# Three seams of a fused attention and two-MoE kernel: root chains moved, one product moved, the last eviction split

## The chip, the cores and the metric

The kernel runs on one core of one Trainium2 chip. The metric is device time in microseconds (us) of one execution, as a median over runs of the same program. TensorE is called PE here, VectorE DVE, ScalarE ACT, GpSimd POOL, and SyncE, which issues the DMAs, SP.

## The reference

```python
B, H, S, D = 4, 8, 576, 64            # q, k, v; 4 * 576 = 2304 tokens, 8 * 64 = 512 features
k_p, v_p = k and v averaged over groups of 8 positions
attn = softmax(q @ k_p.T / sqrt(D))
x = (attn @ v_p) as [2304, 512]
rms = sqrt(mean(x * x, axis=-1) + 1e-6)
xn = x / rms * rms_g
x = (silu(xn @ w_gate) * (xn @ w_val)) @ w_out        # first stage, 512 -> 1536 -> 512
out = ((x @ w_a) * (x @ w_b)) @ w_out2                # second stage, 512 -> 1536 -> 512
```

All inputs and the output are float32; the weights arrive as float64 words and are narrowed on the chip.

## The kernel before

The matrix products run in a rounded 32-bit format. An operand is split into a high part (a cast, on ACT) and a low part (a subtraction, on DVE or POOL), and a product is three matmuls: high by low, high by high, low by high. The matmuls of the large products have 512 columns.

**First stage.** The 2304 tokens are cut into five tiles of 512, 256, 512, 512 and 512 tokens, called tiles 1 to 5 here. A tile runs 12 blocks, one per 128 of the 1536 hidden features. A block is 12 matmuls for the gate `g` (L649), 12 for the value `v` (L649), and the output product `acc` of the block before (L662, 12 matmuls; in tile 2 L670, 8 matmuls). ACT turns `g` into `ht` by silu (L1233). DVE multiplies it by `v` (L1241), which frees the one PSUM bank of `v`. ACT casts it to `hh` (L1250), and DVE subtracts to `hl` (L1251). `ht` has one buffer from tile 3 on. Behind the last block stand two output products in a row, those of blocks 10 and 11 (blocks count from 0), and then the first `g` of the next tile, whose input `xf` is split into `xh` and `xl` (L635, L636) as soon as the last `v` has read the old ones.

**The attention beside it.** The attention of the next tile is worked in steps between these matmuls, in units of 256 tokens. Steps `A5` to `A8` are scores and softmax, `V3` to `V8` the products with the values. A unit ends in a root chain: PE sums the squares (`sq` by L445, or `ms` by L515 and L516), DVE finds the inverse root in three Newton steps (L478 to L493), and scales `xf` by it (L529). In tile 2 the root is found in a narrow form, made into a diagonal matrix `dg` (L464) and spread by PE (`rb`, L472) ahead of the scaling. There the order of the steps is a written list, `SECOND`; in tiles 3 and 4 a list of steps, `SIDE`, is dealt out evenly over 48 places, four for each block (L1206 to L1211). Until tile 5 a scheduler then places each instruction on its engine; in tile 5 and the second stage they stand as they are written.

**Second stage.** Seven products per group (`group`, L1030) go through banks X, Y and Z. The last product of a group, which adds into X, is put off into the next group (`flush`, L1064). `out_block` (L1110) multiplies the hidden features, read back from DRAM, by `w_out2`: for each of the first ten feature blocks three matmuls into each of six banks, then the last two blocks bank by bank, each bank evicted to `ev` and stored (L1136 to L1145). The very last `flush` stands in the first out_block, behind the second bank.

Of the kernel before, what the change touches and what calls it, by code (L numbers as in the profile page):

```python
# [17 lines left out]
P = 128  # L18
UNIT = 256
TILES1 = [512, 256, 512, 512, 512]  # L20
SLICE = 768
# [25 lines left out]
""".split()  # L47
SECOND = """
A4.0 =r0 -r1 r2 -r3 r4 -r5 V3.0 r7 =r6 =r8 -V3.1 =V3.2 N0 =V3.3 A4.1 -N1
=A4.2 A4.3 A4.4 =V3.4 V3.5 -A4.5 =V4.0 . =V4.1 =V3.6 -V4.2 =V4.3 V4.4 V4.5 V3.7 =V4.6  # L50
. =V4.7 . . .
""".split()


# [9 lines left out]
def attention_moe_moe2(  # L64
# [14 lines left out]
    nc = tc.nc  # L79
# [32 lines left out]
    for t0, n in starts(TILES1):  # L112
# [9 lines left out]
        out=mask, in_=mask, pattern=[[P, NV], [-SP, H]], compare_op=ALU.is_ge,  # L122
# [3 lines left out]
        out=mask, in_=mask, pattern=[[-P, NV], [SP, H]], compare_op=ALU.is_ge,  # L126
# [412 lines left out]
    def merge(*lists):  # L539
        keyed = []  # L540
        for order, steps in enumerate(lists):
            for i, st in enumerate(steps):
                keyed.append(((i + 0.5) / len(steps), order, i, st))
        return [st for _, _, _, st in sorted(keyed, key=lambda r: r[:3])]
# [134 lines left out]
    def dest(u):  # L679
        t = u * UNIT  # L680
        for idx, (t0, n) in enumerate(starts(TILES1)):
            if t0 <= t < t0 + n:
                def get():
                    if idx not in xf_t:
                        new_xf(idx)
                    return xf_t[idx][:, :, t - t0:t - t0 + UNIT]
                return get

    A = [score_steps(u) for u in range(NU)]
    V = [value_steps(u, dest(u)) for u in range(NU)]  # L690
    loads, prep = zip(*(prep_steps(b) for b in range(B)))
# [60 lines left out]
    for u in range(5):  # L752
# [3 lines left out]
    SIDE = [  # L756
        [],
[lambda t=t: token(t) for t in SECOND],
        A[5] + list(prep[2][9:]) + prep[3] + merge(A[6], V[5]) + V[6],
        A[7] + merge(A[8], V[7]) + V[8],  # L760
    ]

    def token(t):
        behind = t[0] if t[0] in "-=" else ""
        key, _, banks = t.lstrip("-=").partition("@")
        boot["alt"] = key[-1] == "!"
        key = key.rstrip("!")
        boot["banks"] = banks.split(",") if banks else []
        boot["on"] = key[0] in "kwtx" or key[:2] in ("A0", "A1", "V0", "V1")
        run(names[key], behind)  # L770
        boot["on"] = False
        boot["banks"] = []
        boot["alt"] = False
# [71 lines left out]
    NS2 = NT // SLICE  # L845
# [164 lines left out]
    def bank(name):  # L1010
        return two["ps"].tile([P, 512], F32, tag="bank", name=name, bufs=8)
# [52 lines left out]
    def flush():  # L1064
        if not pending:
            return
        f, s, X, c00 = pending.pop()
        product(X, f, A11, s, "t4", False, True)
        nc.vector.tensor_mul(c00, c00, X[:, :HALF])
        store(f, s, 0, c00)  # L1070
# [32 lines left out]
    def prepare():  # L1103
        if todo:
            s, f = todo.pop(0)
            if s == 0:
                out_weights(f)
            hidden_of(s, f)

    def out_block(s):  # L1110
        accs = []

        def add(f, i):
            if f == 0:
                accs.append(bank(f"o_{s}_{i}"))
            wh, wl = WO[f]
            hh, hl = HO[s, f]
            sub = slice(i * P, (i + 1) * P)
            for j, (x, y) in enumerate(((hh, wl), (hh, wh), (hl, wh))):
                nc.tensor.matmul(  # L1120
                    accs[i], x[:, sub], y, start=(f == 0 and j == 0), stop=(f == NF - 1 and j == 2),
                )

        NA = SLICE // P
        for f in range(NF - 2):
            for i in range(NA):
                add(f, i)
                if f == 0 and s == 0 and i == 1:
                    flush()
                    later.close()  # L1130
                    two["r"] = ctx.enter_context(
                        tc.tile_pool(name="o3", bufs=1, side="right", reuse_waits="tile")
                    )
            prepare()
        prepare()
        for i, acc in enumerate(accs):  # L1136
            for f in range(NF - 2, NF):
                add(f, i)
            ev = two["o"].tile([P, 512], F32, tag="ev2", name=f"ev_{s}_{i}", bufs=3)
            if i % 2 == 0:  # L1140
                nc.scalar.copy(ev, acc)
            else:
                nc.vector.tensor_copy(ev, acc)
            t0 = s * SLICE + i * P
            nc.sync.dma_start(out=out[t0:t0 + P, :], in_=ev)  # L1145
        prepare()

# [2 lines left out]
    def second_phase():  # L1150
# [37 lines left out]
        for s in range(NS2):  # L1188
            out_block(s)

    last_act = [None]
    for idx, (ph, t0, n) in enumerate(work):
# [70 lines left out]
        for c, acc in enumerate(accs):  # L1263
            if last_tile:
                if c == 0:
                    last_x = x_p.tile([P, KD, 512], F32, tag="xf", name="last_x")
                ev = last_x[:, c]
            else:
                ev = ev_p.tile([P, 512], F32, tag="ev", name="ev")
# [45 lines left out]
```

## Time and profile before

| | |
|---|---|
| median of 3 runs | 1023.58 us (1022.65 to 1023.66) |
| the profiled execution, its own time | 1024.57 us |
| its span, first to last instruction | 1022.80 us |
| PE busy | 980.8 us, 96% of the span |
| DVE, ACT, POOL busy | 612.5, 451.7 and 399.6 us |
| mean granted PE clock | 0.985 of full speed |
| chain that ended last | PE 81%, DVE 12%, DMA 3%, issue 2%, ACT 1% |

The chain that ended last is followed back from the last instruction, each step to what released it. It is on PE for most of the span, so what can be won lies where PE waits, where it runs at half its clock, and in what follows its last matmul. Such places are found in the table of PE's waits, in the stretches with their granted clock, and in the timeline. A matmul's printed end is modelled: while PE runs without a pause, 512-column matmuls start 0.23 us apart and are printed as 0.39 us long.

### The profile page before, as it was taken

The numbers are of one execution on the slowest core, as the hardware profiler recorded it, in microseconds if no ns is written. First come the engines' busy times: TensorE is split into PE (matmuls) and PEld (weight loads), VectorE is DVE, ScalarE is ACT, GpSimd is POOL, SyncE is SP. The second block draws the span as 40 slices with busy tenths as digits, with TensorE's granted clock in tenths as the row PEclk, the third lists the DMA queues.
The fourth block names the chain that finished last, engine by engine and source line by source line (L and its number), as shares of the span: only waits on it lengthen the run. The fifth ranks groups of instructions, "written<-read, shape, count | busy, mean of one in ns | idle before, by whom it ended". The sixth has DMA issues, their size and how long they took to land.

```text
span 1022.8 us, 13568 instructions
## 1 busy us (share of the span) xinstructions
PE 980.8 (96%) x4920; PEld 845.7 (83%) x4920; DVE 612.5 (60%) x966; ACT 451.7 (44%) x848; POOL 399.6 (39%) x324
## 2 busy tenths in 40 slices
PE   4988999999999989999999999999999999999998
PEld 3776676788888877888788899999999999888886
DVE  6898966775634764463628759766776665222221
ACT  3845662454535445444445445444444434321211
POOL 6476672533343433343348611533344333310000
PEclk9889999999999999999999999999999999999999
DMA  8556544320100001000111133443444345643431
GB/s 228 156 175 195 176 141 107 113 70 1 42 8 14 1 6 57 1 1 1 42 44 60 42 115 128 125 160 119 148 146 127 126 137 183 193 136 124 140 115 67
DMA packets 82802, 101.55 MB, mean 99 GB/s; under 512 B 24112, under 2 KB 63024, under 8 KB 82736
## 3 DMA queue, kind: packets, MB, share of 16 engines
q1 hardware_dynamic: 82736, 100.69, 31.7%
q8 instruction: 39, 0.64, 0.3%
q14 instruction: 27, 0.22, 0.1%
HBM read 73.93 MB, written 26.74 MB: 98 GB/s over the span
## 4 chain that ended last, share of the span: by engine, by line
PE 81%; DVE 12%; DMA 3%; issue 2%; ACT 1%; SPq 0%; DVEq 0%; ACTq 0%
PE o L1120 15%; PE X L1019 14%; PE v L649 10%; PE g L649 10%; PE acc L662 9%; PE Y L1019 7%; PE acc L670 4%; PE Z L1019 3%; PE xT L399 2%; PE g L799 2%; PE v L799 2%; PE sc L318 1%; DVE wf L596 1%; DVE wf L599 1%; DMA kv<-in_k_dram 1%
## 5 line engine op out<-in xcount | busy, mean ns | idle before, releaser
L621 POOL TENSOR_TENSOR wl<-wf,wh 128x512 fp32r<-128x512 f32 x144 | 193.6, 1351 | 242.6 <-ACT wh L620 230.3
L620 ACT CAST wh<-wf 128x512 fp32r<-128x512 f32 x156 | 94.9, 618 | 77.9 <-PE v L649 31.8
L1098 DVE TENSOR_TENSOR hl<-hf,hh 128x768 fp32r<-128x768 f32 x36 | 34.3, 958 | 95.5 <-ACT hh L1097 95.4
L1120 PE MATMUL o<-woh,hl 128*128 128x512 f32 x216 | 85.8, 397 | 0.0
L1120 PE MATMUL o<-woh,hh 128*128 128x512 f32 x216 | 85.0, 393 | 0.0
L1120 PE MATMUL o<-wol,hh 128*128 128x512 f32 x216 | 84.7, 392 | 0.0
L606 POOL TENSOR_TENSOR w<-w,st 128x512 int32<-128x512 int32 x24 | 31.9, 1328 | 115.8 <-DVE w L599 114.6
L649 PE MATMUL v<-xh,wl 128*128 128x512 f32 (+1 forms) x192 | 72.7, 379 | 1.8 <-DVE ht L1241 1.8
L649 PE MATMUL g<-xh,wl 128*128 128x512 f32 (+1 forms) x192 | 73.0, 380 | 0.0
L649 PE MATMUL g<-xh,wh 128*128 128x512 f32 (+1 forms) x192 | 70.2, 366 | 0.0
L649 PE MATMUL g<-xl,wh 128*128 128x512 f32 (+1 forms) x192 | 70.2, 366 | 0.0
L649 PE MATMUL v<-xl,wh 128*128 128x512 f32 (+1 forms) x192 | 69.9, 364 | 0.0
L649 PE MATMUL v<-xh,wh 128*128 128x512 f32 (+1 forms) x192 | 69.7, 363 | 0.0
L1097 ACT CAST hh<-hf 128x768 fp32r<-128x768 f32 x36 | 29.8, 834 | 89.8 <-PE o L1120 83.0
L670 PE MATMUL acc<-ht,wf 128*128 128x256 f32 (+1 forms) x208 | 67.5, 466 | 1.2 <-DVE ht L813 0.7
L606 POOL TENSOR_TENSOR wf<-wf,st 128x512 int32<-128x512 int32 x36 | 52.9, 1476 | 39.0 <-DVE wf L599 17.3
L1241 DVE TENSOR_TENSOR ht<-ht,v 128x512 f32<-128x512 f32 (+1 forms) x48 | 29.6, 617 | 64.1 <-PE v L649 60.0
L662 PE MATMUL acc<-hh,wl 128*128 128x512 f32 x144 | 57.5, 399 | 3.8 <-ACT hh L1250 3.8
L1233 ACT ACTIVATE ht<-g 128x512 f32<-128x512 f32 (+1 forms) x48 | 26.1, 544 | 77.8 <-PE g L649 71.7
L662 PE MATMUL acc<-hl,wh 128*128 128x512 f32 x144 | 57.0, 396 | 0.1
L1027 ACT COPY p<-X 128x384 f32<-128x384 f32 x36 | 17.2, 478 | 90.2 <-PE X L1019 90.2
L662 PE MATMUL acc<-hh,wh 128*128 128x512 f32 x144 | 56.8, 394 | 0.0
(208 smaller groups left out, 2713.2 us busy)
## 6 DMA issues: line engine op xcount, KB each, us to landing
hf<-h SPq DMA_DIRECT2D x36, 384.0 KB
st<-in_moe_w_out_dram SPq DMA_DIRECT2D x24, 512.0 KB
h<-u SPq DMA_DIRECT2D x36, 192.0 KB
h<-p SPq DMA_DIRECT2D x36, 192.0 KB
st<-in_moe_w_gate_dram SPq DMA_DIRECT2D x12, 512.0 KB
st<-in_moe_w_val_dram SPq DMA_DIRECT2D x12, 512.0 KB
st<-in_moe_w_a_dram SPq DMA_DIRECT2D x12, 512.0 KB
st<-in_moe_w_b_dram SPq DMA_DIRECT2D x12, 512.0 KB
```

What stands on the lines that cost most here:

```text
L606: nc.gpsimd.tensor_tensor(out=bits, in0=bits, in1=low, op=ALU.add)
L620: nc.scalar.copy(wh, wf[ph, f, i])
L621: (nc.vector if boot["alt"] else nc.gpsimd).tensor_sub(wl, wf[ph, f, i], wh.bitcast(F32))
L649: nc.tensor.matmul(bank[:, :n], w[:, c, :], x[:, c, cols], start=(i == 0), stop=(i == 3 * KD - 1),)
L662: nc.tensor.matmul(accs[c][:, cols], w[:, c, :], x[:, :n], start=(f == 0 and i == 0 and cols.start == 0), stop=(f == NF - 1 and i == 2),)
L670: nc.tensor.matmul(accs[c][:, cols], wf[0, f, 2][:, c, :], ht[:, :cols.stop - cols.start], start=(f == 0 and cols.start == 0), stop=(f == ...
L799: nc.tensor.matmul(bank[:, :n], w[:, c, :], x[:, c, cols], start=(c == 0 and i == 0), stop=(c == KD - 1 and i == len(terms) - 1),)
L1019: nc.tensor.matmul(dst[:, :HALF], w[:, c0 + c, :], x[:, c, :], start=(start and i == 0), stop=(stop and i == 5), skip_group_check=True,)
L1097: nc.scalar.copy(hh, hf)
L1098: nc.vector.tensor_sub(hl, hf, hh.bitcast(F32))
L1120: nc.tensor.matmul(accs[i], x[:, sub], y, start=(f == 0 and j == 0), stop=(f == NF - 1 and j == 2),)
L1241: nc.vector.tensor_mul(ht[:, :m], ht[:, :m], vb[:, :m])
```

## The change

It has three parts. In tile 2 the last two units' steps trade places in the written list: the sum of unit 4 (`V4.6`) now stands ahead of the scaling of unit 3 (`V3.7`), and the scaling of unit 4 (`V4.7`) one place later. In tiles 3 and 4 six empty steps are put behind the list, so that 48 and 36 steps become 54 and 42 over the same 48 places. In the first out_block the last `flush` stands behind the third bank instead of the second. The last eviction of all is done in halves of 256 columns, the first by ACT, which also issues its store, the second by DVE with SP's store. In the changed program DVE's half waits for ACT's.

```diff
 SECOND = """
 A4.0 =r0 -r1 r2 -r3 r4 -r5 V3.0 r7 =r6 =r8 -V3.1 =V3.2 N0 =V3.3 A4.1 -N1
-=A4.2 A4.3 A4.4 =V3.4 V3.5 -A4.5 =V4.0 . =V4.1 =V3.6 -V4.2 =V4.3 V4.4 V4.5 V3.7 =V4.6
-. =V4.7 . . .
+=A4.2 A4.3 A4.4 =V3.4 V3.5 -A4.5 =V4.0 . =V4.1 =V3.6 -V4.2 =V4.3 V4.4 V4.5 =V4.6 V3.7
+. . =V4.7 . .
 """.split()
...
-        A[5] + list(prep[2][9:]) + prep[3] + merge(A[6], V[5]) + V[6],
-        A[7] + merge(A[8], V[7]) + V[8],
+        A[5] + list(prep[2][9:]) + prep[3] + merge(A[6], V[5]) + V[6] + [lambda: None] * 6,
+        A[7] + merge(A[8], V[7]) + V[8] + [lambda: None] * 6,
...
-                if f == 0 and s == 0 and i == 1:
+                if f == 0 and s == 0 and i == 2:
                     flush()
...
+            t0 = s * SLICE + i * P
+            if s == NS2 - 1 and i == NA - 1:
+                nc.scalar.copy(ev[:, :256], acc[:, :256])
+                nc.scalar.dma_start(out=out[t0:t0 + P, :256], in_=ev[:, :256])
+                nc.vector.tensor_copy(ev[:, 256:], acc[:, 256:])
+                nc.sync.dma_start(out=out[t0:t0 + P, 256:], in_=ev[:, 256:])
+                continue
```

On PE in tile 2, blocks 10 and 11, before (`rb` spreads the root of a unit, `sq` sums the squares of unit 4; `acc` is the output product):

```order
L670 MATMUL acc_1555<-ht,wf_0_8_1085 128x256
L472 MATMUL rb_2183<-dg_2065,ones 128x256
L649 MATMUL g<-xh,wl_2133 128x256
...
L445 MATMUL sq_2203<-ones,ss_2098 128x2 x2
L649 MATMUL v<-xh,wl_2175 128x256
...
L670 MATMUL acc_1555<-ht,wf_0_9_1190 128x256
L472 MATMUL rb_2243<-dg_2221,ones 128x256
L649 MATMUL g<-xh,wl_2200 128x256
```

The same place now:

```order
L670 MATMUL acc_1555<-ht,wf_0_8_1085 128x256
L445 MATMUL sq_2183<-ones,ss_2098 128x2 x2
L649 MATMUL g<-xh,wl_2133 128x256
...
L472 MATMUL rb_2221<-dg_2065,ones 128x256
L649 MATMUL v<-xh,wl_2175 128x256
...
L670 MATMUL acc_1555<-ht,wf_0_9_1190 128x256
L649 MATMUL g<-xh,wl_2218 128x256
...
L472 MATMUL rb_2265<-dg_2201,ones 128x256
L649 MATMUL v<-xh,wl_2240 128x256
```

The sum `sq` moved ahead by the 12 gate matmuls of block 10, and the last `rb` moved behind the 12 gate matmuls of block 11.

On DVE at the end of tile 3, before (`sl` is the low part of the squares that PE sums into `ms`, `nr` the root, `xf` the next tile's input):

```order
L508 CAST sh_3273<-ss_3149 128x256
L1241 TENSOR_TENSOR ht<-ht,v 128x512
L509 TENSOR_TENSOR sl_3274<-ss_3149,sh_3273 128x256
L1251 TENSOR_TENSOR hl<-ht,hh 128x512
L478 TENSOR_SCALAR ss_3149<-ms_3294 128x256
...
L529 TENSOR_TENSOR xf_2750<-xf_2750,nr_3297 128x4x256
L1241 TENSOR_TENSOR ht<-ht,v 128x512
L636 TENSOR_TENSOR xl<-xf_2750,xh 128x512 x2
L1251 TENSOR_TENSOR hl<-ht,hh 128x512
```

The same place now:

```order
L508 CAST sh_3202<-ss_3078 128x256
L509 TENSOR_TENSOR sl_3203<-ss_3078,sh_3202 128x256
L1247 TENSOR_TENSOR ht<-ht,v 128x512
L478 TENSOR_SCALAR ss_3078<-ms_3220 128x256
...
L529 TENSOR_TENSOR xf_2707<-xf_2707,nr_3223 128x4x256
L1247 TENSOR_TENSOR ht<-ht,v 128x512
L1257 TENSOR_TENSOR hl<-ht,hh 128x512
L1247 TENSOR_TENSOR ht<-ht,v 128x512
L636 TENSOR_TENSOR xl<-xf_2707,xh 128x512 x2
L1257 TENSOR_TENSOR hl<-ht,hh 128x512
```

One pair of `ht` and `hl` more stands between the scaling and the split of `xf`: the chain moved ahead by a block. On PE its sum `ms` stood behind `v` of block 10 and the output product after it; now it stands right behind `v` of block 9, which is 48 matmuls of 512 columns earlier. In tile 4 `ms` stood in the middle of `v` of block 10; now it stands ahead of `g` of block 9, 54 matmuls earlier, and three pairs of `ht` and `hl` follow the scaling. Early in tile 4, ACT now has the exponent of unit 7's softmax, with a table load on either side, ahead of the silu of block 1; it stood behind it.

## Rows read from the trace of the kernel before

**Rows 1.** Waits of PE by what ended them: total us, times, longest us

```profile
PE rb L472 <- DVE dg L464: 4.9, 3, 2.0
...
PE acc L662 <- ACT hh L1250: 3.8, 2, 3.3
...
PE eT L367 <- DVE e L342: 1.7, 2, 1.0
PE X L1019 <- DVE p L1058: 1.4, 1, 1.4
```

**Rows 2.** Windows: us, busy (instructions) by engine, PEclk, DMA share, GB/s

```profile
254.10:257.40 3.30, 3.30 (x15) 3.12 (x15) 1.22 (x1) 0.00 (x0) 0.00 (x0) 0.50 0.00 0
380.40:383.70 3.30, 3.30 (x10) 2.48 (x9) 2.25 (x4) 1.61 (x3) 1.60 (x1) 0.50 0.14 55
```

**Rows 3.** PE timeline, end of tile 2: start us, us, engine, line, instruction

```profile
246.34 0.59 PE L472 MATMUL rb<-dg,ones 128*128 128x256 f32 x2
...
248.19 0.50 PE L445 MATMUL sq<-ones,ss 128*128 128x2 f32 x4
...
253.96 1.07 PE L472 MATMUL rb<-dg,ones 128*128 128x256 f32 x2 [2.00 <-DVE dg L464]
...
257.40 0.34 PE L649 MATMUL v<-xh,wl 128*128 128x256 f32 x1
```

**Rows 4.** Timeline of DVE, the last root chain of tile 2

```profile
248.73 0.16 DVE L478 TENSOR_SCALAR ba<-sq 128x4 f32<-128x4 f32 x1 [0.54 <-PE sq L445]
...
253.33 0.48 DVE L464 TENSOR_SCALAR dg<-ident,br 128x128 f32<-128x128 f32 x2
```

**Rows 5.** Timeline of PE at the seam of tiles 3 and 4

```profile
365.46 0.39 PE L662 MATMUL acc<-hh,wl 128*128 128x512 f32 x1
...
368.19 0.28 PE L515 MATMUL ms<-sl,ones 128*128 128x256 f32 x1
...
376.36 0.39 PE L662 MATMUL acc<-hl,wh 128*128 128x512 f32 x1
380.01 0.47 PE L662 MATMUL acc<-hh,wl 128*128 128x512 f32 x1 [3.26 <-ACT hh L1250]
...
384.43 0.39 PE L649 MATMUL g<-xh,wl 128*128 128x512 f32 x1
```

**Rows 6.** Timeline of DVE, the last root chain of tile 3

```profile
368.63 0.42 DVE L478 TENSOR_SCALAR ss<-ms 128x256 f32<-128x256 f32 x1 [0.24 <-PE ms L516]
...
372.55 1.55 DVE L492 TENSOR_TENSOR y<-y,ss 128x256 f32<-128x256 f32 x1
...
376.95 1.22 DVE L529 TENSOR_TENSOR xf<-xf,nr 128x1024 f32<-128x1024 f32 x1
```

**Rows 7.** Timeline of POOL, the low part of one split weight

```profile
372.53 1.29 POOL L621 TENSOR_TENSOR wl<-wf,wh 128x512 fp32r<-128x512 f32 x1 [2.01 <-ACT wh L620]
```

**Rows 8.** Timeline of PE at the seam of tiles 4 and 5

```profile
496.95 0.47 PE L662 MATMUL acc<-hh,wl 128*128 128x512 f32 x1 [0.51 <-ACT hh L1250]
...
500.16 0.39 PE L649 MATMUL g<-xh,wl 128*128 128x512 f32 x1
```

**Rows 9.** Timeline of PE where the out-projection begins

```profile
865.14 0.40 PE L1120 MATMUL o<-wol,hh 128*128 128x512 f32 x1
...
865.84 0.40 PE L1120 MATMUL o<-wol,hh 128*128 128x512 f32 x1
```

**Rows 10.** Timeline of all engines at the end

```profile
1018.74 0.69 DVE L1143 COPY ev<-o 128x512 f32<-128x512 f32 x1 [2.10 <-PE o L1120]
1019.46 0.33 SPq L1145 DMA_DIRECT2D out_dram<-ev  x1
```

**Rows 11.** Groups by form, half-wide evictions, busy us, mean ns

```profile
L1273 DVE COPY ev<-acc 128x256 f32<-128x256 f32 x2 | 0.8, 418 | 1.9 <-PE g L649 1.9
...
L1271 ACT COPY ev<-acc 128x256 f32<-128x256 f32 x2 | 0.7, 366 | 1.8 <-DMA x<-ev 1.8
```

**Rows 12.** DMA in 40 slices of 1018 to 1023 us: GB/s

```profile
GB/s 410 181 0 0 0 82 295 442 344 426 360 148 0 0 0 0 0 0 197 410 360 426 360 312 33 0 0 0 0 0 0 0 0 0 0 0 0 0 0 0
```

More of the change, by code (lines that the diff above doesn't have):

```diff
@@ L1143, in out_block @@
                 nc.vector.tensor_copy(ev, acc)
-            t0 = s * SLICE + i * P
             nc.sync.dma_start(out=out[t0:t0 + P, :], in_=ev)
```

## The prediction

> **What bounds the kernel now.** I read the chain that ended last first: PE carries 81% of it, and PE is busy for 96% of the span, so a change gains only where PE waits, runs slowly, or has finished. Then the table of PE's waits, for the four that touch the edited places [rows 1]: the last spreading `rb` of tile 2 waits 2.0 us for the diagonal matrix `dg`, an output product at the end of tile 3 waits 3.3 us for `hh`, a transpose early in tile 4 waits 1.0 us for the softmax, and the last `flush` waits 1.4 us for DVE to read bank X. Third, the windows with the granted clock [rows 2]: right behind the waits of tiles 2 and 3 PE was granted 0.50, which is 1.2 of 2.4 GHz. So these two waits cost their idle time and a slow stretch besides. Last, the timelines of PE and DVE around each place.
>
> A printed idle counts from a modelled end. Matmuls that follow without a pause start 0.23 us apart, since three take 0.70 us [rows 9], but are printed as 0.39 us long [rows 5]; so I add 0.16 us to an idle.
>
> **Tile 2.** The last `rb` waits 2.00 + 0.16 = 2.16 us. From its start at 253.96 to the first value matmul at 257.40 it and 12 gate matmuls take 3.44 us; the same work before it, 246.34 to 248.19, took 1.85 us [rows 3]. The slow clock thus cost 1.59 us, and the place 3.75 us. Nothing is added or removed by the trade: `sq`, both `rb` and both scalings remain. The sum `sq` moves from 248.19 to 246.34, 1.85 us earlier. Its DVE chain, L478 at 248.73 to the end of `dg` at 253.81, is 5.08 us [rows 4]; with the scaling of unit 3 now in its middle (1.22 us, the length of L529 [rows 6]) it would end at 248.73 - 1.85 + 5.08 + 1.22 = 253.2. The last `rb` moves behind the gate of block 11. Without the wait that gate starts at 253.96 - 2.16 = 251.8 and takes about 1.6 us, so `rb` is due at 253.4. The wait goes, with 0.2 us to spare; were the chain 1.3 us longer by one POOL split, 1.1 us of the 3.75 would return. Next in line are the splits `xh` and `xl`, which lie beside two output products and were waited for by nobody. I take 3.75, range 2.65 to 3.75.
>
> **The end of tile 3.** PE waits 3.26 + 0.16 = 3.42 us at 380.01. The 12 matmuls from there to 384.43 take 4.42 us, an ordinary output product 2.73 us (365.46 to 368.19), so the slow clock and restart cost 1.69 us [rows 5]. Together 5.11 us. The cause stands in DVE's queue: the root chain holds DVE from 368.63 to 378.17, 9.54 us [rows 6], and block 11's `ht` is queued behind it, though its `v` had long been done. In the new order the sum stands 48 matmuls earlier, 48 x 0.227 = 10.9 us. Even with one more pair of `ht` and `hl` in it (0.7 us each, as a 512-wide DVE pass [rows 10]) the chain ends near 378.2 - 10.9 + 1.4 = 368.7, ahead of the end of the last `v`, which lies one output product ahead of 376.6, at 373.9. What is late next is the ordinary sequence `ht`, `hh`, `hl`, three passes of 0.7 us, beside block 10's output product of 2.73 us: hidden. I take the whole 5.11.
>
> **The end of tile 4.** The wait is 0.51 + 0.16 = 0.67 us for `hh`; from 496.95 to 500.16 the product takes 3.21 instead of 2.73 us, as `hl` is late too [rows 8]. That is 1.15 us. The chain moves by 54 matmuls, 12.2 us, and the whole is gained.
>
> **Inside tiles 3 and 4.** The same attention steps, with the same instructions, now fill about seven eighths of the places. The transpose's wait early in tile 4 was 1.0 + 0.16 = 1.16 us. The exponent now runs ahead of the silu, so the softmax is ready sooner; but that silu and the weight casts behind it come later, and the low part that POOL makes for the gate of block 2 (1.29 us [rows 7]) may be what PE waits for instead. Bounds: 1.16 us gained to 0.13 lost (1.29 in place of 1.16). I take 0.4 gained, nearer the loss because both ends of that trade stand on the path.
>
> In tile 3 the sum `ms` now follows right behind a `v`. Its input leaves PE 2.72 us earlier, and two ACT and three DVE operations lie between, about 0.4 us each with their hand-overs, about 2.3 us. One DVE operation that meets a POOL split would make PE wait: at 372.55 L492 took 1.55 us where its neighbours took 0.42, and POOL's split ran from 372.53 to 373.82 [rows 6, 7]. Between 0 and 1.29 us; I take 0.45 lost. By the Trainium skill's page "SBUF — State Buffer", section "Who interferes with whom", a DVE operation with two SBUF inputs and a GpSimd operation that reads SBUF take turns for a whole instruction; the row agrees. By that rule a block has three splits to meet wherever the chain stands, so moving it cannot shorten it and 0.45 stays; without it this loss would be nil.
>
> For smaller waits of this kind at the other moved steps I take 0.3 lost, between 0 and 1.3 (one more split on the path).
>
> **The last flush.** The wait ends when DVE has read X, which does not depend on the third projection bank. Three matmuls, 0.70 us [rows 9], move into a wait of 1.4 + 0.16 = 1.56 us. The operands of the third bank are those of the first two, so it waits for nothing new. Gain 0.70; 0.86 us of wait remains.
>
> **The last eviction.** Before: DVE's copy from 1018.74, 0.69 us, then the store's issue at 1019.46 [rows 10]; the bytes move in slices 18 to 24 of the 40, 1020.25 to 1021.1 [rows 12]. Now ACT's half takes 0.37 us and DVE's 0.42 us [rows 11], one after the other since DVE's half waits for ACT's, with a hand-over of about 0.05: the second store is issued 0.37 + 0.05 + 0.42 - 0.69 = 0.15 us later. But only half of the bytes, about 0.4 of 0.85 us, still have to move then. Net gain 0.25. The trace shows no DMA issued by ACT; bounds are 0.4 gained (no hand-over, no wait between the halves) and 1.6 lost (ACT's store takes longer by as much as a whole one of SP's, from issue to last byte, 1019.46 to 1021.1). I take 0.25, as a store of the same kind is the nearest row.
>
> By the Trainium skill's page "PSUM — Partial Sum Buffer", section "PSUM bank collisions raise a hardware error", two engines must not be in one PSUM bank at a time, two readers included. No row here shows two readers in one bank. By that rule the halves cannot overlap, and the gain is the 0.25 above; if they could, it would be 0.28 + 0.4, some 0.7.
>
> **The sum.** 3.75 + 5.11 + 1.15 + 0.4 + 0.70 + 0.25 = 11.36 gained, 0.45 + 0.3 = 0.75 lost: 10.6 us net. PE is the bound to the end, so what is won early is kept. Against the profiled execution's own 1024.57 that gives 1013.9. The profile ran 1.0 us above the median of the runs, 1023.58, and against that median it is **1012.9 us**.
>
> **Rivals.**
> *The middle pays.* Fuller places make PE wait inside tiles 3 and 4 at three to five new spots of about 1 us, one of them long enough for another slow stretch of 1.6 us: 4 us lost in all, 1016.9. For it: DVE and POOL hold each other up, and steps of one chain now stand closer. Against it: the transpose's 1.0 us is the only wait of PE above 0.2 us that its table has inside tiles 3 and 4 [rows 1], with the same steps nearly as close.
> *The slow stretches stay.* If the clock falls at those places for another reason than the idle time, only the idle is won: 1012.9 + 1.59 + 1.69 = 1016.2. Against it: both stretches begin within 0.5 us of the end of a wait of more than 2 us.
> *The chain goes ahead of the gate* (slower). The moved chains stand ahead of the next block's `ht` in DVE's queue, and `v` has one bank. If a chain outlasts the time to the next `v` (13.6 us in tile 3, 10.9 us in tile 4, counted in matmuls of 0.227 us from `ms`), PE stops for `v` and falls to half its clock: 2.2 to 3.4 us and 1.6 us at each of the four root chains, 15 to 20 us in all, less the 10.6: 1028 to 1033, about 1030. It turns the whole to a loss only when all four overrun. The chain of tile 3 took 9.5 us with three meetings with POOL, so each would need two to four more.
> *It does not do what it says.* The scheduler could leave the steps where they were: 1023. The order shows them moved, so only an equal wait elsewhere could bring this.
>
> **Chances.** Forecast 0.72, the middle pays 0.16, slow stretches stay 0.05, slower 0.03, no effect 0.04. The forecast's own range is 1010.8 to 1015: with every uncertain term at its good end it is 0.75 + 0.75 + 0.15 = 1.65 lower, 1011.3, less half of the runs' spread of 1.0, 1010.8; with the bad ends of tile 2 (1.1) and of the inside (0.5 + 0.85) nearly 1015 is reached, less than all of 2.45 being likely at once. With the middle-pays case the range is 1010.8 to 1016.9. A measurement of this kernel can tell 0.2%, about 2 us, from no change. Faster takes the first three cases, 0.93; same 0.04; slower 0.03.
>
> **What would show it.** Right: no wait of PE above 1 us at the last `rb` of tile 2 and at the two seams, no stretch near half the granted clock behind the first 100 us, the wait at the last `flush` near 0.8 us, and the last store's bytes ending about 0.3 us nearer to PE's last matmul. Wrong: a PE wait for `ms`, `wl` or `v` of over 2 us inside tiles 3 and 4, or a slow stretch there; or a first ACT store that takes microseconds longer than SP's.

## The result, and the profile after

The changed kernel takes 1012.6 us as a median (1011.5 to 1014.5), against 1023.6 us for the kernel before on the same chip: a ratio of 0.9892, with a 95% interval of 0.9875 to 0.9908, or 11.0 us. On a second chip the ratio was 0.9890 (0.9872 to 0.9908). The forecast was 1012.9 us within 1010.8 to 1016.9.

The profiled execution took 1014.52 us, with a span of 1012.75 us, 10.05 us less than the span of before. These are the rows of its page that answer to the table of before: instructions and busy time of PE, and the granted clock in 40 equal slices.

```profile
span 1012.8 us, 13575 instructions
...
PE 976.4 (96%) x4920; PEld 842.3 (83%) x4920; DVE 610.0 (60%) x966; ACT 452.0 (45%) x849; POOL 402.9 (40%) x324
...
PEclk8799999999999999999999999999999999999999
```

Behind the first two slices no slice is below 9. The table of PE's waits (total us, times, longest us) answers to [rows 1]:

```profile
PE rb L472 <- DVE dg L464: 3.0, 2, 2.0
...
PE X L1019 <- DVE p L1058: 0.7, 1, 0.7
...
PE eT L367 <- DVE el L380: 0.3, 1, 0.3
```

The wait for `hh` is gone from the table. One of the three waits for `dg` is gone; the two that are left lie in the first tile. The long wait for `e` early in tile 4 is gone, a new one of 0.3 us for `el` has come, and the `flush` waits half as long. The windows at the three seams, in the columns of [rows 2], show the full clock:

```profile
253.70:257.00 3.30, 3.30 (x24) 3.11 (x23) 2.07 (x3) 1.97 (x5) 1.29 (x1) 1.00 0.01 2
371.50:374.80 3.30, 3.30 (x16) 2.75 (x15) 3.06 (x6) 3.30 (x7) 0.05 (x1) 1.00 0.01 2
485.00:488.30 3.30, 3.30 (x17) 2.72 (x16) 3.14 (x6) 2.57 (x5) 0.00 (x0) 1.00 0.00 0
```

PE at the end of tile 2 answers to [rows 3]:

```profile
245.36 1.89 PE L670 MATMUL acc<-ht,wf 128*128 128x256 f32 x8
247.09 0.50 PE L445 MATMUL sq<-ones,ss 128*128 128x2 f32 x4
...
253.98 0.59 PE L472 MATMUL rb<-dg,ones 128*128 128x256 f32 x2
...
259.10 0.58 PE L649 MATMUL g<-xh,wl 128*128 128x512 f32 x1
```

The last `rb` waits for nothing. From this `acc` (244.61 before, 245.36 now) to the first gate of tile 3 (262.14, 259.10) it is 13.74 us instead of 17.53. DVE has `dg` ready 2.0 us ahead of the `rb`, in the chain that answers to [rows 4]:

```profile
247.63 0.16 DVE L478 TENSOR_SCALAR ba<-sq 128x4 f32<-128x4 f32 x1 [0.71 <-PE sq L445]
...
249.78 1.21 DVE L529 TENSOR_TENSOR xf<-xf,rb 128x1024 f32<-128x1024 f32 x1
...
251.48 0.48 DVE L464 TENSOR_SCALAR dg<-ident,br 128x128 f32<-128x128 f32 x2
```

PE at the seam of tiles 3 and 4, the first matmul of the two output products and of the next gate, answers to [rows 5]; the root chain of DVE, now 10.5 us earlier against the end of the tile, to [rows 6]:

```profile
371.47 0.39 PE L662 MATMUL acc<-hh,wl 128*128 128x512 f32 x1
...
376.91 0.39 PE L649 MATMUL g<-xh,wl 128*128 128x512 f32 x1
```

```profile
355.71 0.42 DVE L478 TENSOR_SCALAR ss<-ms 128x256 f32<-128x256 f32 x1
356.17 1.14 DVE L481 TENSOR_SCALAR nr<-ss 128x256 int32<-128x256 int32 x1
...
359.06 1.40 DVE L493 SCALAR_TENSOR_TENSOR nr<-y,nr 128x256 f32<-128x256 f32 x1
...
362.33 1.40 DVE L492 TENSOR_TENSOR y<-y,ss 128x256 f32<-128x256 f32 x1
...
364.22 1.23 DVE L529 TENSOR_TENSOR xf<-xf,nr 128x1024 f32<-128x1024 f32 x1
365.36 0.68 DVE L1247 TENSOR_TENSOR ht<-ht,v 128x512 f32<-128x512 f32 x1
```

Two output products in a row take 5.44 us, about twice the 2.73 of one; before it was 10.56. The chain has three stretched passes again (1.14, 1.40 and 1.40 us) and takes 9.7 us with one `hl` pass now inside it (9.5 before): it hardly got shorter, it stands where nothing is queued behind it that PE needs soon. The seam of tiles 4 and 5, in the place of [rows 8], runs through as well:

```profile
484.89 0.39 PE L662 MATMUL acc<-hh,wl 128*128 128x512 f32 x1
...
490.33 0.39 PE L649 MATMUL g<-xh,wl 128*128 128x512 f32 x1
```

The end, in the place of [rows 10]:

```profile
1008.43 0.40 PE L1120 MATMUL o<-woh,hl 128*128 128x512 f32 x1
1008.91 0.37 ACT L1142 COPY ev<-o 128x256 f32<-128x256 f32 x1 [0.85 <-PE o L1120]
1009.31 0.38 ACTq L1143 DMA_DIRECT2D out_dram<-ev  x1
1009.31 0.42 DVE L1144 COPY ev<-o 128x256 f32<-128x256 f32 x1 [2.50 <-ACT ev L1142]
1009.76 0.33 SPq L1145 DMA_DIRECT2D out_dram<-ev  x1
```

DVE's half waits for ACT's. From the start of the last matmul to the end of the span it was 4.55 us and is 4.32 us.

Taken between the same matmuls of the two profiles, the 10.05 us are:

| part | gain, us | term of the prediction |
|---|---|---|
| start to the end of tile 2 | -0.75 | none |
| end of tile 2 | 3.79 | 3.75 |
| inside tile 3 | -0.64 | -0.45, and part of -0.3 |
| seam of tiles 3 and 4 | 5.12 | 5.11 |
| inside tile 4 | 1.15 | 0.4, and part of -0.3 |
| seam of tiles 4 and 5 | 1.16 | 1.15 |
| second stage to the last `flush` group | -0.65 | none |
| the `flush` and the out-projection | 0.64 | 0.70 |
| behind the last matmul | 0.23 | 0.25 |

The first line is no work of the change: in the twelve profiles, with those below, in which the first tile is unedited, the same matmul of tile 2 starts between 242.5 and 245.5 us, in no order with the edits. The 0.65 us of the second stage is a spread of that kind too; from its first product to the last `flush` group it took 265.5 to 267.0 us over the profiles.

### The profile page after: what moved, and what is told of

Read it like the earlier page. It is cut to its first block, busy times and chain, and to the rows that moved or that the text cites. A ratio compares the mean times of both kernels' runs of the same rounds, so it can differ in the third digit from the quotient of the medians.

```text
span 1012.8 us, 13575 instructions
## 1 busy us (share of the span) xinstructions
PE 976.4 (96%) x4920; PEld 842.3 (83%) x4920; DVE 610.0 (60%) x966; ACT 452.0 (45%) x849; POOL 402.9 (40%) x324
## 4 chain that ended last, share of the span: by engine, by line
PE 81%; DVE 11%; DMA 3%; issue 2%; ACT 2%; SPq 0%; DVEq 0%; ACTq 0%
PE o L1120 15%; PE X L1019 14%; PE v L649 10%; PE g L649 10%; PE acc L662 9%; PE Y L1019 7%; PE acc L670 3%; PE Z L1019 3%; PE xT L399 2%; PE v L799 2%; PE g L799 1%; PE sc L318 1%; DVE wf L596 1%; DVE wf L599 1%; DVE kp L189 1%
## 5 line engine op out<-in xcount | busy, mean ns | idle before, releaser
L621 POOL TENSOR_TENSOR wl<-wf,wh 128x512 fp32r<-128x512 f32 x144 | 196.6, 1373 | 230.7 <-ACT wh L620 221.0
L1098 DVE TENSOR_TENSOR hl<-hf,hh 128x768 fp32r<-128x768 f32 x36 | 34.5, 963 | 95.0 <-ACT hh L1097 95.0
```

Of the source, the lines that this page charges most:

```text
L621: (nc.vector if boot["alt"] else nc.gpsimd).tensor_sub(wl, wf[ph, f, i], wh.bitcast(F32))
L1098: nc.vector.tensor_sub(hl, hf, hh.bitcast(F32))
```

## The experiments

**One part alone: tile 2.** The kernel before with the trade in `SECOND` only.

```diff
-=A4.2 ... =V4.3 V4.4 V4.5 V3.7 =V4.6
-. =V4.7 . . .
+=A4.2 ... =V4.3 V4.4 V4.5 =V4.6 V3.7
+. . =V4.7 . .
```

> The kernel before with the trade in tile 2's list alone. My theory: the wait of PE for dg at the last rb (2.16 us) and the stretch at half the clock behind it (1.59 us) both go, 3.75 us in all, about 1019.8 against 1023.6; the waits at the ends of tiles 3 and 4 and the half-clock stretch at 380 us stay as they were. Rival, the slow stretch has another cause than the idle time: only 2.2 us go and a stretch at half the clock still stands in tile 2, about 1021.4. Rival, the root chain is late again in the new place: a wait of about 1 us at rb remains, about 1021.

Measured: 1021.42 us against 1024.53, a ratio of 0.9976 (0.9965 to 0.9986), so 2.5 us (1.4 to 3.6); the two medians alone lie 3.1 us apart. In the trace the end of tile 2 takes 13.74 us, the same as in the changed kernel; wait and slow stretch are gone there, and those of the end of tile 3 are as before. The gain in time, however, falls short of the 3.75 us: by the ratio it lies nearer to the 2.2 us that the idle time alone gives. Why, the next run began to show.

**One part alone: the empty steps.** The kernel before with the six empty steps behind both lists.

```diff
-        A[5] + ... + merge(A[6], V[5]) + V[6],
-        A[7] + merge(A[8], V[7]) + V[8],
+        A[5] + ... + merge(A[6], V[5]) + V[6] + [lambda: None] * 6,
+        A[7] + merge(A[8], V[7]) + V[8] + [lambda: None] * 6,
```

> The kernel before with the six empty steps behind the lists of tiles 3 and 4 alone. My theory: the root chain leaves DVE's queue ahead of the last block's ht, so the wait at the end of tile 3 and its slow stretch go (5.1 us) and the wait at the end of tile 4 (1.15 us); the inside of the tiles gives 0.5 us back as in the changed kernel (0.64 lost in tile 3, 1.15 gained in tile 4): 6.8 us, about 1016.8 against 1023.6. Tile 2 keeps its wait and its half-clock stretch at 254 us. Rival, the gains of the seams hang on the trade in tile 2 (its other order shifts what DVE has to do in tile 3): less than 4 us. Rival by my recorded sum, in which the inside loses 0.35 us: 5.9 us, 1017.7, and the trace has the waits inside that say so.

Measured: 1017.64 us against 1024.53, 0.9940 (0.9924 to 0.9956), 6.2 us (4.5 to 7.8). The trace has the seams at 5.44 us each and the inside as in the changed kernel (112.41 and 108.00 us): the gain doesn't hang on tile 2. But tile 2 itself, unchanged here, brought a surprise. Its wait of 2.00 us for `dg` is there, and the window behind it has the full clock:

```profile
253.90:257.20 3.30, 3.30 (x27) 3.25 (x28) 1.22 (x1) 0.89 (x2) 0.29 (x1) 1.00 0.01 2
```

27 matmuls stand in it where [rows 2] has 15, and the end of tile 2 takes 15.99 us instead of 17.53.

**The empty steps in front.** They make the steps stand as close, but leave the root chains at the end.

```diff
-        A[5] + ... + V[6],
-        A[7] + merge(A[8], V[7]) + V[8],
+        [lambda: None] * 6 + A[5] + ... + V[6],
+        [lambda: None] * 6 + A[7] + merge(A[8], V[7]) + V[8],
```

> The kernel before with the six empty steps put ahead of the lists of tiles 3 and 4 instead of behind them: the steps stand as close as in the changed kernel, but the root chain of tile 3 begins at the old place (ms behind the output product, 48 matmuls ahead of the tile's end) and that of tile 4 six matmuls later than before. My theory, it is the place of the chain in DVE's queue that counts: the wait of about 3.4 us and the half-clock stretch at the end of tile 3 stay, and the wait at the end of tile 4 grows from 0.67 to about 2 us; 1024 to 1027. Rival, the closer steps or the smaller number of steps in the early places bring the gain: 1017 to 1020.

Measured: 1023.65 us against 1024.53, 1.0000 (0.9986 to 1.0014). PE's rows at the two seams:

```profile
378.91 0.47 PE L662 MATMUL acc<-hh,wl 128*128 128x512 f32 x1 [3.26 <-ACT hh L1250]
```

```profile
495.56 0.47 PE L662 MATMUL acc<-hh,wl 128*128 128x512 f32 x1 [0.96 <-ACT hh L1250]
```

The first is the wait of [rows 5] to the hundredth, with its slow stretch; the second grew from 0.51 to 0.96, less than the 2 us expected. So it is the place of the chain in DVE's queue that counts and not how close the steps stand. The wait of 1.0 us early in tile 4 is absent here as well: that one does come from the closer steps.

**Does an idle PE bring the slow stretch by itself?** Waits put into tile 5, far from any seam.

```diff
             step()
+            if last_tile:
+                hl = h_p.tile([P, 512], F32R, tag="hl", name="hl")
+                for _ in range({1: 9, 4: 10, 7: 11, 10: 14}.get(f, 0)):
+                    nc.vector.tensor_copy(hl[:, :m], vb[:, :m])
             nc.vector.tensor_mul(ht[:, :m], ht[:, :m], vb[:, :m])
```

> The changed kernel with extra copies of v by DVE ahead of ht in tile 5, 9, 10, 11 and 14 of them in blocks 1, 4, 7 and 10, so that the next v waits about 0.9, 1.5, 2.1 and 3.9 us (worked out from 0.60 us from one DVE pass to the next, 5.67 us from one v to the next). The output is unchanged. My theory: a slow stretch follows a long enough idle time of PE wherever it lies, and costs about 1.6 us more: half the clock behind the wait of 3.9 us and probably behind that of 2.1, none behind 0.9 and 1.5; the time 8.4 us of waits and 1.6 to 3.2 us of slow clock longer than the changed kernel's, 1022.6 to 1024.2. Rival, the slow stretches came from what runs at the seams (narrow products, the change of tile): full clock in all of tile 5, 1021.

Measured: 1039.94 us, far more than expected. A copy took 0.72 us, not 0.60, and in the last two of the blocks DVE had other steps to finish first, so the waits are longer than planned: 2.0, 2.7, 7.5 and 7.6 us with the 0.16 us added. The first two lines are PE's rows at the first and third wait, the others, from the windows of that profile, the stretches behind all four:

```profile
507.20 0.47 PE L649 MATMUL v<-xh,wl 128*128 128x512 f32 x1 [1.83 <-DVE ht L1251]
...
569.62 0.77 PE L649 MATMUL v<-xh,wl 128*128 128x512 f32 x1 [7.29 <-DVE ht L1251]
```

```profile
508.60:511.80 3.20, 3.20 (x9) 2.46 (x9) 0.18 (x1) 1.54 (x3) 3.07 (x3) 0.50 0.00 0
...
535.90:539.20 3.30, 3.05 (x7) 2.48 (x8) 2.58 (x4) 1.66 (x3) 1.94 (x2) 0.50 0.00 0
...
569.70:573.30 3.60, 3.60 (x9) 2.83 (x10) 3.14 (x5) 2.27 (x5) 1.38 (x1) 0.50 0.00 0
...
603.60:607.40 3.80, 3.80 (x9) 3.03 (x10) 0.69 (x1) 2.78 (x6) 2.77 (x3) 0.50 0.00 0
```

All four are at half the clock. Tile 5 with its end takes 26.85 us longer; the waits are 19.73 of them and the slow clock 7.1, or 1.8 a stretch. So the rival falls: the stretch follows the idle time and not what runs at a seam. The expectation that a wait of 1.5 us brings none was not put to the test, since no wait came out below 2.0. By the Trainium skill's page "TensorE: Matmul & The Clock Gate", section "HAM oscillation — how this bites in real kernels", a wait can throttle PE again so that the work behind it starts cold; these four rows agree. That it does not do so each time is shown by the row of tile 2 with the full clock above and by the profiles further below.

**Three and twelve empty steps instead of six.** The diff is that of three; with twelve the number alone differs.

```diff
-... + V[6] + [lambda: None] * 6,
-... + V[8] + [lambda: None] * 6,
+... + V[6] + [lambda: None] * 3,
+... + V[8] + [lambda: None] * 3,
```

> The changed kernel with three empty steps instead of six: the sum ms of tile 3 stands 24 matmuls (5.5 us) earlier than in the kernel before instead of 48, that of tile 4 30 instead of 54. My theory, all that counts at the seams is that the chain has left DVE's queue when the last v has been read: the chain of tile 3 then ends 5.5 us less 1.4 us for one more pair of ht and hl earlier than before, about 374, when the last v ends at 373.9; so both seams take 5.44 us as in the changed kernel, with less than 0.5 us of wait. Inside, the new wait of 0.34 us for el in tile 3 need not come back, since it hangs on the place of single steps: tile 3 between 111.7 and 112.4 us, tile 4 between 108 and 109.1. Rival, the gain grows with the number of empty steps: a wait of 1.5 us or more at the end of tile 3, half way to the 3.4 of before.

> The changed kernel with twelve empty steps instead of six: ms of tile 3 stands 84 matmuls earlier than in the kernel before, that of tile 4 90, and the steps of tile 3 fill four fifths of the places. My theory: the seams have nothing left to give, 5.44 us each as in the changed kernel. The inside decides, and steps that stand closer cost a little there: tile 3 112.4 to 113.5 us, tile 4 108 to 109. Rival, the middle pays (a rival of my prediction): three or more waits of about 1 us inside tiles 3 and 4, one of them with a half-clock stretch, 3 us or more lost.

Measured: 1013.74 and 1014.69 us, one execution each. The seams take 5.44 us in both, as with six. Inside, tile 3 takes 111.77 us with three, 112.37 with six and 113.59 with twelve; tile 4 takes 107.98, 107.98 and 108.05. So twelve came out just above the 112.4 to 113.5 us expected. Most of the difference in tile 3 is one wait of PE, absent with three, here with six and with twelve; with the 0.16 us added it is 0.50 of 0.60 us and 1.31 of 1.82:

```profile
338.44 0.44 PE L367 MATMUL eT<-ident,e 128*128 128x128 f32 x2 [0.34 <-DVE el L380]
```

```profile
332.04 0.44 PE L367 MATMUL eT<-ident,e 128*128 128x128 f32 x2 [1.15 <-DVE el L380]
```

So the gain at the seam is a step and not a slope: it is whole as soon as the chain has left the queue, which three steps (24 matmuls) already bring, and six and twelve only cost more inside. "The middle pays" is a rival that is true in kind, at 0.6 us with six steps and 1.9 with twelve, not at 4.

**The flush two banks later, and both halves of the last store on SP.**

```diff
-                if f == 0 and s == 0 and i == 2:
+                if f == 0 and s == 0 and i == 4:
...
-                nc.scalar.dma_start(out=out[t0:t0 + P, :256], in_=ev[:, :256])
+                nc.sync.dma_start(out=out[t0:t0 + P, :256], in_=ev[:, :256])
```

> Two independent edits of the changed kernel. First, the last flush stands behind the fifth projection bank instead of the third. The wait left there is 0.72 + 0.16 = 0.88 us, and six more matmuls take 1.4 us: my theory says the wait goes and the place gains 0.88 us; the rival says that the wait follows the flush, since DVE's pass is itself late. Second, SP issues both halves of the last store instead of ACT the first. My theory, the gain came from the half of the bytes that is left to move, not from the second queue: 4.3 us from the start of the last matmul to the end of the span, as in the changed kernel (4.32; 4.55 before). Rival, ACT's queue is what helped: SP's first issue of 0.33 us delays nothing, but the two stores move one behind the other in one queue, 4.55 us or more.

Measured: 1014.04 us, one execution. PE at the last `flush`, and the end:

```profile
859.72 0.39 PE L1120 MATMUL o<-woh,hl 128*128 128x512 f32 x1
859.95 0.34 PE L1019 MATMUL X<-xh_t,bl 128*128 128x384 f32 x1
```

```profile
1007.99 0.40 PE L1120 MATMUL o<-woh,hl 128*128 128x512 f32 x1
1008.47 0.37 ACT L1142 COPY ev<-o 128x256 f32<-128x256 f32 x1 [0.85 <-PE o L1120]
1008.86 0.33 SPq L1143 DMA_DIRECT2D out_dram<-ev  x1
...
1009.32 0.35 SPq L1145 DMA_DIRECT2D out_dram<-ev  x1
```

The `flush` follows without a wait. From the last group's product ahead of it to the last matmul of the kernel it is 152.63 us, against 153.62 in the changed kernel: 0.99 us gained. From the last matmul to the end of the span it is 4.34 us, against 4.32 with ACT's queue. So ACT's queue has no part in the gain at the end. What is left is the half of the bytes that goes ahead: from the last issue to the end of the span it was 3.34 us and is 2.99 in the changed kernel.

**A further seam, in the first tile.** A step of its written list moved, the same cure at another place.

```diff
-... p3! -c a4 -v4a s3.0 =c -p4 -v4b s3.1! =c
-=o3 =g5a =p5! =c =h4 c -c s4.0! ...
+... p3! -c a4 -v4a s3.0 =c -p4 -v4b s3.1! h4 =c
+=o3 =g5a =p5! =c c -c s4.0! ...
```

> The changed kernel with one step of the first tile's written list moved: the product ht of block 4 stands four bit passes of the weights (L596, L599) earlier in DVE's queue. In the changed kernel PE waits 2.77 + 0.16 us there at 86.6 us, with a half-clock stretch of 3.41 us behind it. The same kind of cause as at the seams: DVE's queue holds back the ht that frees the bank of v. Theory A, PE is the bound here as everywhere: ht comes about 2.5 us earlier, the slow stretch goes, 4.1 us gained, about 1015.5 less than 1023.6 by the changed kernel's 11.0 and 4.1: 1008.5. Theory B, in the first tile the conversion of the weights is the bound (ACT waits 1.2 to 2.0 us for each load of weight words here): the wait comes back at 113 us, where PE waits 1.15 us for wl, as one of about 4 us, and 0 to 1.6 us are gained.

Measured: 1012.99 us against 1025.35, 0.9880 (0.9860 to 0.9900), which can't be told from the changed kernel's 0.9892. The wait of 2.77 us at 86.6 us is gone, and so is the slow stretch. In their place PE waits at two others, and then, as it did before, for `wl`:

```profile
87.68 0.50 PE L799 MATMUL g<-xh,wl 128*128 128x512 f32 x1 [0.95 <-ACT ht L807]
...
94.87 0.50 PE L799 MATMUL v<-xh,wl 128*128 128x512 f32 x1 [0.72 <-DVE ht L813]
...
111.89 0.50 PE L799 MATMUL g<-xh,wl 128*128 128x512 f32 x1 [1.13 <-DVE wl L621]
```

The last of these came at 113.33 us in the changed kernel; over the profiles with the old list it came at 112.9 us in the mean (110.9 to 113.8), and at 111.9 and 111.1 in the two with the new one. So about 1.4 us is left of 4.1, and even that is not clear of the spread: the one profile with the old list that has no slow stretch behind its 2.77 us is the one at 110.9 us, earlier than both. Theory B names the right size but not the place: no wait of 4 us came at 113 us, the waits came back earlier than it said. The waits that came back show that PE alone is not the bound in the first tile; which other engine is was not tried.

**The kernel before, profiled twice more.** No edit.

> The kernel before itself, for one more profile of it. Its wait of 2.0 us in tile 2 was followed by a stretch at half the clock in one profile of it and by none in two profiles of kernels with the same tile 2. My theory: the wait stands close to what lets the clock fall, so the same code shows the stretch in some executions only, and the end of tile 2 takes 17.5 us with it or 16.0 without; the longer wait at the end of tile 3 has its stretch each time. Rival, the stretch belongs to the kernel before alone, since the order of the instructions in the two others differs later on: 17.5 us again.

> The kernel before once more, for a further profile. Two profiles of it have the half-clock stretch behind the wait in tile 2 and the end of tile 2 at 17.5 us; two kernels with the same instructions there have the same wait, no stretch, and 16.0 us. If the stretch comes in some executions only, this profile may show either, and 16.0 us would settle it; 17.5 us would leave it to the times. The end of tile 3 is expected to have its stretch again, 10.6 us. Rival, the stretch belongs to this kernel: 17.5 us.

Measured: 1025.97 and 1018.73 us. The first has the slow stretch in tile 2 (17.49 us), the one at the end of tile 3, and a third behind the last `flush`, which waited 1.87 us there:

```profile
254.00:257.30 3.30, 3.30 (x17) 3.30 (x17) 1.22 (x1) 0.81 (x2) 0.00 (x0) 0.50 0.01 2
...
868.40:871.60 3.20, 3.20 (x10) 2.82 (x9) 1.66 (x3) 0.58 (x1) 0.00 (x0) 0.50 0.83 282
```

The second has none of them. These are PE's two waits, and the windows behind them:

```profile
251.87 0.67 PE L472 MATMUL rb<-dg,ones 128*128 128x256 f32 x2 [2.01 <-DVE dg L464]
...
376.39 0.47 PE L662 MATMUL acc<-hh,wl 128*128 128x512 f32 x1 [3.26 <-ACT hh L1250]
```

```profile
252.00:255.30 3.30, 3.30 (x27) 3.25 (x28) 1.22 (x1) 0.89 (x2) 0.32 (x1) 1.00 0.01 2
376.40:379.10 2.70, 2.70 (x11) 2.05 (x12) 2.54 (x5) 1.91 (x4) 1.21 (x1) 1.00 0.00 0
```

These two waits are the same to 0.01 us, and the clock is full. The end of tile 2 takes 16.01 us, the seam of tiles 3 and 4 9.12. That settles it for these two places: the idle time is a property of the program, the slow stretch behind it one of the execution. It also refutes the expectation, held in both texts, that the end of tile 3 has its stretch each time. The two profiles come from two chips, but the chip does not decide it: on the second one the same program also ran at 1025.31 us, with a mean granted clock of 0.989 instead of 0.993. What does decide it was not tried.

**What the runs pointed to, together.** The changed kernel with three empty steps, the `flush` behind the fifth bank and `ht` of block 4 moved in the first tile; beside it the changed kernel itself.

```diff
-... -v4b s3.1! =c
-=o3 =g5a =p5! =c =h4 c -c s4.0! ...
+... -v4b s3.1! h4 =c
+=o3 =g5a =p5! =c c -c s4.0! ...
...
-... + V[6] + [lambda: None] * 6,
-... + V[8] + [lambda: None] * 6,
+... + V[6] + [lambda: None] * 3,
+... + V[8] + [lambda: None] * 3,
...
-                if f == 0 and s == 0 and i == 2:
+                if f == 0 and s == 0 and i == 4:
```

> The changed kernel with what the other runs pointed to: three empty steps instead of six, the last flush behind the fifth bank, and the product ht of block 4 of the first tile four bit passes earlier on DVE. Expected against the changed kernel: 0.6 us from tile 3, 0.9 to 1.0 from the flush, and 0.5 to 1.8 from the first tile, 2.0 to 3.4 us together; about 1010 where the kernel before takes 1023.6. Rival, the start of the first tile is bound by the weight conversion: only 1.5 us.

> The changed kernel itself, beside the kernel before and the version above on one chip. By the terms as the traces have them it is 11.1 us faster than a run of the kernel before that has the slow stretch in tile 2, and 9.5 us faster than one that has not; the median between these, 0.989 to 0.991.

Measured on one chip, where the kernel before took 1024.98 us: 1009.99 us, 0.9856 (0.9843 to 0.9870), and the changed kernel 1012.96, 0.9890 (0.9872 to 0.9908). The version is 3.0 us faster than the changed kernel by the medians, within the 2.0 to 3.4 expected, and the two intervals do not overlap. Its parts in the trace are tile 3 at 111.76 us and 152.62 us from the last group to the last matmul, as each had alone.

## Why the prediction was right

**The mechanisms.** All four places did what was forecast. The waits at the last `rb`, at both seams and half of that at the `flush` are gone, no chain holds back the gate, and nothing new is late behind the seams. The runs with one part alone gave 2.5 and 6.2 us, 8.6 together; the flush and the end add about 0.6 (below), which leaves 1.8 to the 11.0 of the whole, within the intervals of the three.

**The step that was mis-sized: a slow stretch counted as a part of its wait.** The prediction read 1.59 and 1.69 us of slow clock from one execution and took them whole. Over the profiles that have the wait of 2.0 us in tile 2 the stretch stood in two of five; behind the 3.26 us of tile 3 it stood in four of five. Its price is 17.5 less 16.0, so 1.5 us, in tile 2, and 10.6 less 9.1, so 1.5, in tile 3; the remainder of the 1.69, about 0.2, is the restart itself. Tile 2 was thus worth 2.26 us without it and 3.79 with it, 2.9 in the mean by two of five; the 2.5 us that the trade alone gained in the times lie between the two. The rival "the slow stretches stay" named the right amounts for an execution without them, but a wrong reason.

**The `flush`, mis-sized in both ways.** Its wait varies: 0.9 to 1.9 us behind the second bank in six profiles, 0.3 to 1.2 behind the third in six. From the last group to the last matmul of the kernel it is 154.03 us in the mean of five profiles with the second bank and 153.63 in the mean of six with the third: 0.40 us and not 0.70. The sixth with the second bank has 156.34, since a slow stretch stands behind its wait of 1.87 us; that the change makes this less likely was counted at nothing. With the fifth bank it is 152.6 us both times. The traces show where the variation comes from, which the prediction took as fixed: DVE's pass on X stands in its queue behind an `hl` (L1098), and DVE sits idle until ACT has cast that one's `hh`, before which ACT itself waited for the load of `hf` (0.34 us in the kernel before). These are the rows of the kernel before, the changed kernel's second profile and the one with twelve empty steps, whose waits at the `flush` are 1.36, 1.24 and 0.26 us:

```profile
866.09 0.98 DVE L1098 TENSOR_TENSOR hl<-hf,hh 128x768 fp32r<-128x768 f32 x1 [0.61 <-ACT hh L1097]
```

```profile
856.01 1.16 DVE L1098 TENSOR_TENSOR hl<-hf,hh 128x768 fp32r<-128x768 f32 x1 [0.99 <-ACT hh L1097]
```

```profile
856.97 1.14 DVE L1098 TENSOR_TENSOR hl<-hf,hh 128x768 fp32r<-128x768 f32 x1
```

Less this idle time the wait is 0.83 us in the mean of six profiles behind the second bank and 0.18 in that of six behind the third. The 0.65 between them are about the 0.70 of the forecast's three matmuls. DVE's idle time took back the rest: it was 0.55 us in the mean of the six profiles with the third bank and 0.31 in the five with the second. Whether that is chance or follows from the change is not shown.

**Tile 2's cover** was ten times larger than thought: the chain was ready 2.0 us early and not 0.2, since it took 4.3 us with the scaling in it. The 5.08 us of before held two passes of L492 of 1.14 and 1.20 us beside POOL's splits, where such a pass is 0.16 long otherwise; I carried these over, and in the new place the only pass stretched by so much as a third of a microsecond was one of L493, to 0.53.

**Inside tiles 3 and 4** I forecast 0.35 us lost, and 0.51 were gained. The wait for `ms` did not come; instead a transpose in tile 3 waited for `el`. In tile 4 the whole 1.15 us came, the good end of the range: neither the later silu nor POOL's split was waited for.

**The chain's length** was rightly kept: 9.7 us against 9.5, with its stretched passes beside POOL's, which ran from 355.86, 358.82 and 361.97 us for 1.29 to 1.47 us each. By the Trainium skill's page "SBUF — State Buffer", section "Who interferes with whom", a DVE operation with two SBUF inputs and a GpSimd operation that reads SBUF take turns; the two passes of 1.40 us above agree. The place of the chain made no difference to the number of stretched passes, three.

**The end** was right: eight profiles with the halves take 4.31 to 4.34 us from the last matmul to the end, six with the whole 4.55 to 4.57, a difference of 0.23 in the mean against the 0.25 forecast. No run had both halves read at once, so that the larger gain of 0.7 stays untried.

The sum came out at 10.6 against 11.0 partly by luck, because errors of both signs were left in it: 0.9 too little inside the tiles, and on the other side 0.3 too much at the `flush` and a slow stretch in tile 2 counted at 1.6 that comes in some executions only. (The sum is 10.61, and 1023.58 less that is 1013.0; the 1012.9 of the prediction is a slip of 0.1.)

## What to carry to other kernels

Where an in-order engine works for two masters, look at what stands behind a long chain in its queue: moving the chain ahead by 24 matmuls won the whole wait, and 48 or 84 won nothing more and cost a little elsewhere. Price a wait of the matrix engine at its idle time, and the slow clock behind it as a chance, read from several profiles of the same program. Ask at each place whether the matrix engine is the bound there: the same cure that paid in full at the seams paid about a third in the first tile, if that.

## What the runs showed of the hardware

The same program ran at 1018.7 and at 1026.0 us with the same waits in tiles 2 and 3. Of the 7.2 us between the two spans 4.6 lie in three stretches at 1.2 GHz (1.5 in tile 2, 1.6 in tile 3, 1.6 behind the `flush`), which follow a wait in one execution and not in the next. They were seen at four places where another profile of the same instructions had none: behind 2.77 us in the first tile (absent in one of twelve profiles), 2.0 us in tile 2, 3.26 us in tile 3 and 1.87 us at the `flush`, where the wait itself varied between 0.93 and 1.87. Over 23 runs of the kernel before beside the first experiments (1020.7 to 1026.6 us) a longer time goes with a lower mean granted clock, with a correlation of -0.83 worked out from the 23 pairs.
